# Polynomial-sketch attention into a SiLU expert layer: paired sketch projections, column-tiled key-value sums, outer products on GpSimd

## The chip, the cores and the metric

One core of a Trainium2 chip runs the whole program. The metric is the device time of one execution in microseconds, and the profile is that of one execution.

## What is computed

Four batches of four heads, 1088 positions, head size 32. Queries and keys are each projected by two sketches of eight rows, and the outer product of the two makes 64 features. Linear attention over these features gives, per head, a numerator and a denominator; the quotient is the input of a two-layer expert with SiLU between (128 to 2048 to 128). The output is float32, 4352 x 128.

```python
a = np.einsum('rd,bhsd->bhsr', S1, x)
b = np.einsum('rd,bhsd->bhsr', S2, x)
phi = np.einsum('bhsi,bhsj->bhsij', a, b).reshape(*x.shape[:-1], r * r)
...
kv = np.einsum('bhsf,bhsd->bhfd', k_p, v)
z = np.sum(k_p, axis=2)
num = np.einsum('bhsf,bhfd->bhsd', q_p, kv)
den = np.einsum('bhsf,bhf->bhs', q_p, z)[..., None] + 1e-06
...
h = x @ w_in
return ((h / (1.0 + np.exp(-h))) @ w_out).astype(np.float32)
```

## The kernel before

**Tiles.** A batch has 34 blocks of 128 numbers a partition; eight groups of four blocks are the main part, and two blocks per batch are left over and gathered into one rest tile (`xR`) for all batches. `CW` is nine groups of 32 columns, 288.

**Keys** (`key_tasks`, L251). VectorE transposes the loaded keys (`kt`, L258), TensorE multiplies them with the first and the second sketch (`proj` by `mm_set`, L220: four float32 matmuls of 288 columns in four column tiles of 32, all 128 rows), VectorE transposes each result back (`tr`, L272). `outer` (L277) makes the 64 features of each head in bfloat16, on GpSimd for batch 1 and on VectorE for the others. `z` (L284), `zt`, `l2` (L293) and `wm` (L297) turn the sums of the keys into the masked weights `WM` for the denominator. `kv` (L308) sums features times values over positions, 18 matmuls with 128 columns of features as weights and two heads' values of 64 columns as the moving operand; `kvm` (L316) masks the blocks of other heads.

**Queries** (`query_tasks`, L348). Transposes (L358, L361), three projections (first sketch, second sketch, `WM`; L220 again), each transposed back (L378); `scale` (L384 to L387) makes the denominator and divides, `outer` (L393) makes the features. These are transposed by TensorE (`pet`, L407, and a ScalarE copy, L413) for the first half of batch 0, and by DMA on SP's queue (`dmat`, L399) for the rest. `num` (L422) multiplies by the key-value block, and ScalarE copies the result into the expert's input (`xcopy`, L429).

**Expert** (`moe_tasks`, L488). 68 steps: `h` (L499, 1024 columns into a pair of PSUM banks), `silu` on ScalarE (L503), `o` (L510, accumulated over the steps of a block of positions), then a VectorE transpose and stores. The steps are 4, 4 and 8 for batch 0, 8 for the four-group blocks, 4 for the two-group blocks, and 4 for the rest.

**Order.** A planner (`Plan`) is given each piece of work with an engine, a cost in microseconds, what it depends on, the bank or buffer it takes and gives back, and a due time; expert step n is due at T0 + STEP x n. It simulates the engines once while the program is built and emits the pieces in the order in which they start, so each engine's queue has a fixed order. Two PSUM banks are for attention (`att`), two for expert outputs (`o`), and two pairs for expert inputs (`h`), which batch 0's projections borrow.

**Idle matmuls.** 24 pieces of two matmuls on zeros (`idler`, L542, 256 columns) are in the plan with a late due time and a cost of 0.3 us, so they go where TensorE would have nothing ready.

**Loads.** Batch 0's keys and queries come on SP's queue, its values, the expert weights and all of batches 1 to 3 on GpSimd's.

Of the kernel before, what the change touches and what calls it, by code (L numbers as in the profile page):

```python
# [12 lines left out]
ALU = mybir.AluOpType  # L13
# [9 lines left out]
class Plan:  # L23
# [11 lines left out]
    def add(self, eng, cost, fn, deps=(), take=None, give=None, ready=0.0, due=None, lag=0.0):  # L35

        t = dict(eng=eng, cost=cost, fn=fn, deps=[d for d in deps if d is not None], take=take,
                 give=give, ready=ready, due=due, lag=lag, succ=[], end=None, floor=self.floor, n=len(self.tasks))
        for d in t["deps"]:
            d["succ"].append(t)  # L40
        self.tasks.append(t)
        return t

    def give(self, t, taker, *others):

        t["deps"] += others
        for d in others:
            d["succ"].append(t)
        t["give"] = taker
# [4 lines left out]
    def start_of(self, t, now):  # L54
        if any(d["end"] is None for d in t["deps"]):
            return None
        at = max([t["ready"], now.get(t["eng"], 0.0)]
                 + [d["end"] + self.hop(d, t) for d in t["deps"]])
        if t["take"]:
            if not self.free[t["take"]]:  # L60
                return None
            at = max(at, min(self.free[t["take"]])[0])
        return at

    def run(self, stretch=1.3):
# [9 lines left out]
        while left:  # L75
# [8 lines left out]
            args = ()  # L84
            if t["take"]:
                slot = min(self.free[t["take"]])
                self.free[t["take"]].remove(slot)
                t["slot"] = slot[1]
                args = (slot[1],)
            t["start"], t["end"] = at, at + t["cost"]  # L90
            now[t["eng"]] = t["end"]
            if t["give"]:
                self.free[t["give"]["take"]].append((t["end"] + 0.2, t["give"]["slot"]))
            left.remove(t)
            t["fn"](*args)

@with_exitstack
def kernel(
# [31 lines left out]
    xp = ctx.enter_context(tc.tile_pool(name="xp", bufs=1))  # L130
    gp = ctx.enter_context(tc.tile_pool(name="gp", bufs=1))
# [39 lines left out]
    WAB = const.tile([P, 2, H, R], FP32, name="WAB")  # L171
# [17 lines left out]
    nc.gpsimd.memset(WAB, 0.0)
# [14 lines left out]

    WA = WAB[:, 0].rearrange("p h r -> p (h r)")
    WB = WAB[:, 1].rearrange("p h r -> p (h r)")
    WB4 = const.tile([P, 4, HR], FP32, name="WB4")
    nc.vector.tensor_copy(out=WB4, in_=_bc(WB, 0, 4))
    L2 = const.tile([P, P], FP32, name="L2")

    xT = [xp.tile([P, 1024], BF16, name=f"xT{b}") for b in range(B)]
    xR = xp.tile([P, B, XN], BF16, name="xR")


    T0, STEP = 13.5, 1.2
    pl = Plan({"att": 2, "h": 2, "o": 2, "g": 6})

    def mm_set(dst, srcT, w, lo, hi):
        for c in range(4):
            nc.tensor.matmul(dst[32 * c: 32 * (c + 1), lo:hi], w, srcT[:, c, lo:hi],  # L220
                             start=True, stop=True, tile_position=(0, 32 * c))

    slots = {"h": [ps.tile([P, 2, 512], FP32, name=f"H{i}") for i in range(2)],
             "o": [ps.tile([P, 512], FP32, name=f"O{i}") for i in range(2)],
             "att": [ps.tile([P, 512], FP32, name=f"A{i}") for i in range(2)],
             "g": [gp.tile([P, 2, 512], BF16, name=f"G{i}") for i in range(6)]}
    POOLED = (1,)
# [3 lines left out]
    def bank(pool, i):  # L231
        return slots[pool][i][:, 0, :] if pool == "h" else slots[pool][i]

    def load(b):
        def lk():
            Kx[b] = tile_x(b, "Kx")
            load_x(nc.gpsimd, Kx[b], k, b, 0, SA)

        def lq():
            Qx[b] = tile_x(b, "Qx")  # L240
            load_x(nc.gpsimd, Qx[b], q, b, 0, SA)
        p = b - 2
        at = {1: (14.0, 16.0, 18.0)}.get(b, (0.0, 0.0, 0.0))
        ks[b]["lk"] = pl.add("POOL", 0.6, lk, [ks[p]["kt"][-1] if p >= 0 else None], lag=3.0, due=4.0 + b)
        qs[b]["lq"] = pl.add("POOL", 0.6, lq, [qs[p]["tr"][-1] if p >= 0 else None], lag=3.0, due=4.1 + b)
        ks[b]["lv"] = pl.add("POOL", 2.2, lambda: load_v(b), [ks[p]["kv"] if p >= 0 else None], lag=4.0, due=4.2 + b)
        if b == 1:
            for st, nm, r in ((ks, "lk", 14.0), (qs, "lq", 16.0), (ks, "lv", 18.0)):
                st[b][nm]["lag"] = r - 8.0

    def key_tasks(b):  # L251
        st = ks[b]
        KT = KTs[b % 2]
        at = ((3.9, 4.7) if b == 0 else (0.0, 0.0))

# [6 lines left out]
        def proj(i, sl=None):  # L262
            if b == 0:
                sl = pr[0]["slot"]
            st[f"p{i}"] = slots["h"][sl][:, i, :] if b == 0 else bank("att", sl)
            mm_set(st[f"p{i}"], KT, (WA, WB)[i], 0, CW)

        def tr(i):
            if i == 0:
                st["ab"] = work.tile([P, 2, NBX, HR], FP32, name="kab", tag="kab")  # L270
                st["kp"] = work.tile([P, NBX * H, R, R], BF16, name="kp", tag="kp")
            nc.vector.transpose(out=st["ab"][:, i].rearrange("p a r -> p (a r)"), in_=st[f"p{i}"][:, 0:CW])  # L272

        def outer(lo, hi):
            a = st["ab"][:, 0, lo:hi, :].rearrange("p a (h r) -> p (a h) r", h=H)
            bb = st["ab"][:, 1, lo:hi, :].rearrange("p a (h r) -> p (a h) r", h=H)
            (nc.gpsimd if b in POOLED else nc.vector).tensor_tensor(out=st["kp"][:, H * lo: H * hi], in0=_bc(a, 2, R),  # L277
                in1=_bc(bb, 1, R), op=ALU.mult)

        def z(sl):  # L280
            st["z"] = bank("att", sl)
# [19 lines left out]
        def kv(lo, hi, sl=None):  # L301
            if lo == 0:
                st["kvp"] = bank("att", sl)
            kpf = st["kp"].rearrange("p (t g) i j -> p t (g i j)", g=H)
            for hp in range(2):
                for t in range(lo, hi):
                    n = P if t < NB else XN
                    nc.tensor.matmul(st["kvp"][:, 64 * hp: 64 * (hp + 1)],  # L308
                                     kpf[:n, t, 128 * hp: 128 * (hp + 1)],
                                     Vb[b][:n, 2 * hp: 2 * hp + 2, t, :],  # L310
                                     start=(t == 0 and hp == 0), stop=(t == NB),
                                     skip_group_check=True)

        def kvm():
            st["KV"] = work.tile([P, 2, 2, D], BF16, name="KV", tag="KV")
# [32 lines left out]
    def query_tasks(b, spans, pe=False, at=0.0, groups=None):  # L348
# [94 lines left out]
        if pe:  # L443
            pl.give(ab[1], pr[0], ab[0])
# [156 lines left out]
```

## Time and profile before

| | before |
|---|---|
| median of 3 runs | 111.0 us (110.92 to 111.31) |
| the profiled execution | 111.13 us |
| its span | 108.8 us |
| TensorE busy | 96.6 us |
| ScalarE busy | 72.5 us |
| VectorE busy | 57.0 us |
| GpSimd busy | 20.3 us |
| mean granted TensorE clock | 0.961 |

The span runs from the first to the last instruction of the core; the rest of an execution's time lies around it. In rows of the trace, PE is TensorE's matmuls, PEld its weight loads, DVE is VectorE, ACT ScalarE, POOL GpSimd, and SP the queue of SyncE. L220 is line 220 of the kernel. A float32 matmul has two records, so a set of four is x8. The ends of matmuls are modelled, and neighbouring ones overlap.

### The profile page before, as it was taken

To read this page: it belongs to the slowest core of one execution; us is meant where nothing else is said; L and a number is where in the kernel's file an instruction comes from. 1 tells how busy PE (TensorE), PEld (TensorE's weight loads), DVE (VectorE), ACT (ScalarE), POOL (GpSimd) and SP (SyncE) were. 2 spreads that over 40 slices of the span, in tenths; PEclk is the share of its full clock that TensorE was granted. 3 is DMA by queue.
4 is the path that set the end of the run, shared out by engine and by line. 5 is a ranking of instruction groups with operands and counts; after the bars stand their busy time and mean duration, and the time that the engine had idled before them with its cause. 6 is when DMAs were issued, how large, how long until landed. Compare 5 with 4: busy or idle time off the path is not lost.

```text
span 108.8 us, 2049 instructions
## 1 busy us (share of the span) xinstructions
PE 96.6 (89%) x771; PEld 50.7 (47%) x771; DVE 57.0 (52%) x119; ACT 72.5 (67%) x90; POOL 20.3 (19%) x43
## 2 busy tenths in 40 slices
PE   0797982999999999999999999999999999989920
PEld 0574751644466533443245334433444444778810
DVE  4631799779879999853686039468710200210110
ACT  4200003553379399978968969786979999999910
POOL 4899022451592430000000000000000000000000
PEclk9999998558999999999999999999999999999996
DMA  1999999899641199224009930600555160051243
GB/s 31 305 181 178 164 353 262 176 195 393 185 68 24 38 147 136 52 31 65 3 0 156 98 65 0 96 0 0 108 83 110 19 96 0 12 85 18 34 58 44
DMA packets 32713, 11.08 MB, mean 102 GB/s; under 512 B 29248, under 2 KB 31296, under 8 KB 32704
## 3 DMA queue, kind: packets, MB, share of 16 engines
q1 hardware_dynamic: 26768, 5.38, 30.4%
q0 software_dynamic: 5376, 5.51, 24.7%
q10 hardware_dynamic: 560, 0.07, 0.4%
q8 instruction: 6, 0.10, 0.4%
q14 instruction: 3, 0.02, 0.1%
HBM read 8.78 MB, written 2.23 MB: 101 GB/s over the span
## 4 chain that ended last, share of the span: by engine, by line
PE 72%; ACT 11%; DVE 8%; issue 2%; DMA 1%; POOL 0%; ACTq 0%; POOLq 0%
PE H_147 L499 14%; PE O_149 L510 12%; PE H_146 L499 11%; PE O_148 L510 10%; PE A_151 L220 6%; PE O_148 L542 5%; PE A_150 L220 4%; ACT G_152 L503 3%; PE A_151 L308 2%; DVE kp L277 2%; PE A_150 L422 2%; ACT G_156 L503 2%; ACT G_153 L503 2%; ACT G_157 L503 2%; ACT G_154 L503 2%
## 5 line engine op out<-in xcount | busy, mean ns | idle before, releaser
L499 PEld LDWEIGHTS <-w_in 128*128 128x128 bf16 x176 | 16.1, 101 | 16.4 <-issue 7.7
L510 PEld LDWEIGHTS <-w_out 128*128 128x128 bf16 x176 | 16.5, 98 | 14.3 <-issue 3.5
L503 ACT ACTIVATE G_154<-H_147 128x1024 bf16<-128x1024 f32 x11 | 11.4, 1036 | 4.9 <-PE H_147 L499 4.8
L503 ACT ACTIVATE G_152<-H_147 128x1024 bf16<-128x1024 f32 x12 | 12.6, 1047 | 2.1 <-PE H_147 L499 2.1
L503 ACT ACTIVATE G_156<-H_147 128x1024 bf16<-128x1024 f32 x11 | 11.4, 1036 | 3.0 <-PE H_147 L499 2.8
L503 ACT ACTIVATE G_155<-H_146 128x1024 bf16<-128x1024 f32 x11 | 11.4, 1034 | 2.5 <-PE H_146 L499 2.5
L503 ACT ACTIVATE G_153<-H_146 128x1024 bf16<-128x1024 f32 x12 | 12.6, 1048 | 0.5 <-PE H_146 L499 0.5
L393 DVE TENSOR_TENSOR qp<-aqs,qabm 128x1024 bf16<-128x1024 f32 (+2 forms) x13 | 11.7, 912 | 0.2
L503 ACT ACTIVATE G_157<-H_146 128x1024 bf16<-128x1024 f32 x11 | 11.5, 1042 | 0.0
L152 POOL DMA_DIRECT2D Vb<-in_v_dram x16 | 8.9, 575 | 9.0 <-PE A_151 L308 3.4
L515 DVE STREAM_TRANSPOSE ot<-O_149 128x256 f32<-128x256 f32 (+1 forms) x6 | 3.5, 582 | 13.2 <-PE O_149 L510 13.2
L515 DVE STREAM_TRANSPOSE ot<-O_148 128x512 f32<-128x512 f32 (+1 forms) x5 | 3.0, 609 | 10.8 <-PE O_148 L510 10.8
L542 PE MATMUL O_148<-zero 128*128 128x256 bf16 x48 | 8.2, 337 | 0.0
L277 DVE TENSOR_TENSOR kp<-kab 128x1280 bf16<-128x1280 f32 (+1 forms) x6 | 8.0, 1341 | 0.0
L378 DVE STREAM_TRANSPOSE qabm<-A_151 128x288 f32<-128x288 f32 (+1 forms) x7 | 3.1, 445 | 6.8 <-PE A_151 L220 6.8
L542 PEld LDWEIGHTS <-zero 128*128 128x128 bf16 x48 | 5.7, 125 | 2.0 <-issue 0.4
L290 ACT ACTIVATE zt<-A_150 128x32 f32<-128x32 f32 x1 | 0.2, 197 | 8.7 <-PE A_150 L284 8.7
L499 PE MATMUL H_147<-xT_141,w_in 128*128 128x256 bf16 (+1 forms) x24 | 5.7, 358 | 0.0
L277 POOL TENSOR_TENSOR kp<-kab 128x512 bf16<-128x512 f32 (+1 forms) x5 | 4.9, 1012 | 3.1 <-DVE kab L272 3.1
L499 PE MATMUL H_146<-xT_141,w_in 128*128 128x256 bf16 (+1 forms) x24 | 5.3, 334 | 0.0
L499 PE MATMUL H_147<-xT_144,w_in 128*128 128x256 bf16 (+1 forms) x24 | 4.8, 307 | 0.4 <-ACT G_156 L503 0.4
L499 PE MATMUL H_147<-xT_143,w_in 128*128 128x512 bf16 x16 | 4.8, 382 | 0.2 <-ACT G_156 L503 0.2
(124 smaller groups left out, 151.1 us busy)
## 6 DMA issues: line engine op xcount, KB each, us to landing
Kx<-in_k_dram POOLq DMA_DIRECT2D x3, 544.0 KB, 9.4
Qx<-in_q_dram POOLq DMA_DIRECT2D x3, 544.0 KB, 4.2
out_dram<-ot SPq DMA_DIRECT2D x24, 64.0 KB, 2.0
Vb<-in_v_dram POOLq DMA_DIRECT2D x8, 72.0 KB, 4.6
Vb<-in_v_dram POOLq DMA_DIRECT2D x8, 64.0 KB, 3.9
w_in<-in_moe_w_in_dram POOLq DMA_DIRECT2D x1, 512.0 KB, 7.8
w_out<-in_moe_w_out_dram POOLq DMA_DIRECT2D x1, 512.0 KB, 10.4
out_dram<-ot SPq DMA_DIRECT2D x14, 32.0 KB, 2.9
```

What stands on the lines that cost most here:

```text
L152: nc.gpsimd.dma_start(t[32 * c: 32 * (c + 1), :, 0:n].rearrange("p h a d -> p h (a d)"), AP(tensor=v.tensor, offset=v[b, 0].offset + KA[c] ...
L220: nc.tensor.matmul(dst[32 * c: 32 * (c + 1), lo:hi], w, srcT[:, c, lo:hi], start=True, stop=True, tile_position=(0, 32 * c))
L277: (nc.gpsimd if b in POOLED else nc.vector).tensor_tensor(out=st["kp"][:, H * lo: H * hi], in0=_bc(a, 2, R), in1=_bc(bb, 1, R), op=ALU.mult)
L308: nc.tensor.matmul(st["kvp"][:, 64 * hp: 64 * (hp + 1)], kpf[:n, t, 128 * hp: 128 * (hp + 1)], Vb[b][:n, 2 * hp: 2 * hp + 2, t, :], start= ...
L378: nc.vector.transpose(out=st["abm"][:, i, lo:hi].rearrange("p a r -> p (a r)"), in_=st[f"p{i}", lo0][:, 32 * lo: 32 * hi])
L393: nc.vector.tensor_tensor(out=qp, in0=_bc(st["aqs"][:, H * lo: H * hi], 2, R), in1=_bc(bq, 1, R), op=ALU.mult)
L422: nc.tensor.matmul(ps[64 * hp: 64 * (hp + 1), :n], kst["KV"][:, hp].rearrange("p h d -> p (h d)"), rhs, start=True, stop=True, tile_positi ...
L499: nc.tensor.matmul(view(cc[jp], i), w_in[:, j * P: (j + 1) * P], x, start=True, stop=True)
L503: nc.scalar.activation(out=cc["g", jp], in_=cc[jp], func=ACT.Silu)
L510: nc.tensor.matmul(cc["o"][:, :n], w_out[:, j, :], view(cc["g", jp], i), start=(j == 0), stop=(j == NJ - 1))
L515: nc.vector.transpose(out=cc["ot"][:, :n], in_=cc["o"][:, :n])
L542: nc.tensor.matmul(slots["o"][idle[1]["slot"]][:, 0:256], zero[:, 0:P], zero[:, 0:256], start=True, stop=True)
```

## The change

- `pairs` replaces the two sketch projections. The weights `WP` hold, for each of two halves of 64 rows (two heads), both sketches of these heads in 32 columns. Eight matmuls of 64 rows and 32 columns are placed at row tile 64p and column tile 32c, and each half p writes a bank of its own. `unpair` transposes one such bank back and writes it into the places of both sketches. The third query projection (`projm`) stays as it was.
- `kv` has the values as weights (32 columns of one head) and 64 columns of features as the moving operand, in four column tiles of 32: 36 matmuls. `kvm` masks the result into two copies, `kvt` turns it round by a TensorE transpose, and `kvc` copies it to SBUF, on ScalarE for batch 0 and on VectorE otherwise.
- `outer` of the keys runs on GpSimd for batches 1, 2 and 3, in five pieces each.
- Attention and expert outputs share four PSUM banks (`s`); a piece may take several. Batch 0's projections use these too.
- Keys and queries of batches 2 and 3 are loaded by SP's queue; their loads are ordered behind the last DMA transpose of the batch two before, and so are the loads of values on GpSimd's queue.
- The plan is made first and emitted afterwards. Idle matmuls are no longer pieces of the plan: `emit` puts them into each planned gap of TensorE up to the planned start of the first expert matmul.
- T0 goes from 13.5 to 14.0, STEP from 1.2 to 1.1. The preparation of the weights moves partly between VectorE and GpSimd.

```diff
+    def emit(self, fill=None, until=0.0):
+        last = 0.0
+        for t in self.tasks:
+            if t["eng"] == "PE":
+                if fill and last < until:
+                    fill(last, min(t["start"], until))
+                last = t["end"]
+            t["fn"](*t["slot"])
...
+    zero = const.tile([P, 256], BF16, name="zero")
     nc.gpsimd.memset(S12, 0.0)
+    nc.vector.memset(zero, 0.0)
...
     for h in range(H):
-        (nc.vector if h < 2 else nc.gpsimd).tensor_copy(
-            out=WAB[D * h: D * (h + 1), :, h, :], in_=ST[:, 0:2 * R].rearrange("p (n r) -> p n r", n=2))
+        nc.vector.tensor_copy(out=WP[D * h: D * (h + 1), :, h % 2, :],
+                              in_=ST[:, 0:2 * R].rearrange("p (n r) -> p n r", n=2))
+        nc.gpsimd.tensor_copy(out=WB4[D * h: D * (h + 1), :, h, :], in_=_bc(ST[:, R:2 * R], 0, 4))
...
-    T0, STEP = 13.5, 1.2
-    pl = Plan({"att": 2, "h": 2, "o": 2, "g": 6})
+    T0, STEP = 14.0, 1.1
+    pl = Plan({"h": 2, "s": 4, "g": 6})
...
+    def pairs(dst, srcT, lo, hi):
+
+        for c in range(4):
+            for p in range(2):
+                nc.tensor.matmul(dst[p][32 * c: 32 * (c + 1), lo:hi], WPf[64 * p: 64 * (p + 1), :],
+                                 srcT[64 * p: 64 * (p + 1), c, lo:hi],
+                                 start=True, stop=True, tile_position=(64 * p, 32 * c))
+
+    def unpair(dst, src, p, lo, hi, cut=0):
+
+        nc.vector.transpose(
+            out=dst[:, 0:2, lo:hi, 2 * R * p: 2 * R * (p + 1)].rearrange("p n a g -> p a n g"),
+            in_=src[:, 32 * lo: 32 * hi])
...
+            ks[b]["lk"] = pl.add("SP", 0.5, lk, [ks[p]["kt"][-1], qs[p]["dm"]], lag=4.0)
+            qs[b]["lq"] = pl.add("SP", 0.5, lq, [qs[p]["tr"][-1], qs[p]["dm"]], lag=4.0)
+            ks[b]["lv"] = pl.add("POOL", 2.2, lambda: load_v(b), [ks[p]["kv"], qs[p]["dm"]], lag=4.0)
...
+        def kv(sl):
+            st["kvp"] = bank[sl]
+            kpf = st["kp"].rearrange("p (t h) i j -> p t h (i j)", h=H)
+            for t in range(NBX):
+                n = P if t < NB else XN
+                for h in range(H):
+                    nc.tensor.matmul(st["kvp"][D * h: D * (h + 1), 0: R * R], Vb[b][:n, h, t, :],
+                                     kpf[:n, t, h, :], start=(t == 0), stop=(t == NB),
+                                     tile_position=(0, D * h))
...
+            st["kvx"] = work.tile([P, 2, R * R], BF16, name="kvx", tag="kvx")
+            nc.vector.tensor_tensor(out=st["kvx"], in0=_bc(st["kvp"][:, 0: R * R], 0, 2),
+                                    in1=_bc(pmask[:, :], 1, R * R), op=ALU.mult)
+
+        def kvt():
+            st["kvb"] = st["kvp"].bitcast(BF16)[:, 512: 512 + P]
+            nc.tensor.transpose(st["kvb"], st["kvx"].rearrange("p g f -> p (g f)"), identb)
...
+        pr = pl.add("PE", 0.55, proj, st["kt"], take=("s", "s"))
...
+        k1 = st["kv"] = pl.add("PE", 0.6, kv, ou + [lv], take=("s",), ready=10.0 if b == 0 else 0.0)
...
+    K0CUTS = [("DVE", 0, 5), ("DVE", 5, 9)]
+    KPOOL = [("POOL", i, min(i + 2, NBX)) for i in range(0, NBX, 2)]
...
     pl.run()
+    t1 = first_h[0]["start"]
+
+
+    idle = slots["h"][1][:, 1, 0:256]
+
+    def fill(lo, hi):
+        step = 0.22 if lo < 5.0 else 0.115
+        for _ in range(max(0, int((hi - max(lo, 1.0) - 0.1) / step))):
+            nc.tensor.matmul(idle, zero[:, 0:P], zero, start=True, stop=True)
+
+    pl.emit(fill, t1)
```

## Rows read from the trace of the kernel before

**Rows 1.** The page: busy time by engine, and the granted clock in 40 slices.

```profile
PE 96.6 (89%) x771; PEld 50.7 (47%) x771; DVE 57.0 (52%) x119; ACT 72.5 (67%) x90; POOL 20.3 (19%) x43
...
PEclk9999998558999999999999999999999999999996
```

**Rows 2.** Windows of 1 us: stretch, length, busy PE, PEld, DVE, ACT, POOL, clock, DMA.

```profile
18.00:19.00 1.00, 0.30 (x2) 0.11 (x1) 0.93 (x3) 0.56 (x2) 0.03 (x1) 0.71 1.18 258
...
24.00:25.00 1.00, 1.00 (x12) 0.43 (x4) 0.97 (x4) 0.82 (x1) 0.17 (x1) 0.50 1.05 391
25.00:26.00 1.00, 1.00 (x11) 0.21 (x10) 0.90 (x4) 0.00 (x0) 0.35 (x1) 0.88 0.98 370
```

**Rows 3.** The chain that ended last, in order of time: start, us, what.

```profile
3.98 5.61 PE O_148 L542 x32
...
19.25 0.61 PE O_148 L407 x4
...
28.83 0.44 PE A_151 L284 x18
...
29.31 0.69 PE A_150 L220 x8
...
35.66 0.84 PE A_151 L308 x18
36.50 0.54 PE H_147 L499 x2
37.03 0.43 PE H_146 L499 x2
37.47 0.62 PE A_150 L220 x8
38.09 0.48 PE A_151 L220 x8
...
58.62 0.84 PE A_151 L308 x18
...
100.83 0.87 ACT G_157 L503
```

**Rows 4.** Timeline of the start: start, length, engine, line, what, idle before.

```profile
4.20 1.39 DVE L258 STREAM_TRANSPOSE KT_88<-Kx 128x576 f32<-128x576 f32 x2 [0.75 <-DMA Kx<-in_k_dram]
...
11.57 0.48 DVE L272 STREAM_TRANSPOSE kab<-H_146 128x288 f32<-128x288 f32 x1 [0.81 <-PE H_146 L220]
...
17.58 0.60 ACT L413 ACTIVATE qt<-O_149 128x512 bf16<-128x512 bf16 x1 [4.43 <-PE O_149 L407]
...
19.65 1.06 PE L499 MATMUL H_147<-xT_141,w_in 128*128 128x256 bf16 x4
```

**Rows 5.** Windows of the idle matmuls (L542) alone: busy PE, PEld, clock, DMA.

```profile
5.50:7.50 2.00, 2.00 (x11) 1.44 (x10) 1.00 1.19 206
...
8.00:9.60 1.60, 1.58 (x14) 1.13 (x11) 1.00 0.92 160
```

**Rows 6.** Windows of ScalarE alone: stretch, length, busy time, clock, DMA.

```profile
26.00:40.00 14.00, 8.82 (x12) 1.00 0.52 117
...
sum 83.05, ACT 68.99; mean ACT 11.50
```

**Rows 7.** Timeline, outer products of keys on GpSimd and VectorE, and two of queries.

```profile
28.44 4.92 POOL L277 TENSOR_TENSOR kp<-kab 128x512 bf16<-128x512 f32 x5 [3.09 <-DVE kab L272]
...
29.02 0.78 DVE L393 TENSOR_TENSOR qp<-aqs,qabm 128x256 bf16<-128x256 f32 x1
...
40.30 0.38 DVE L393 TENSOR_TENSOR qp<-aqs,qabm 128x256 bf16<-128x256 f32 x1
40.60 2.62 DVE L277 TENSOR_TENSOR kp<-kab 128x1280 bf16<-128x1280 f32 x2
```

**Rows 8.** DMA issues: KB each, median us from issue to landing.

```profile
Kx<-in_k_dram POOLq DMA_DIRECT2D x3, 544.0 KB, 9.4
...
qt<-qp SPq DMA_TRANSPOSE x11, 3.1
```

More of the change, by code (lines that the diff above doesn't have):

```diff
@@ L56, in start_of @@
             return None
[L57 to L60, printed above, removed]
+        at = max([t["ready"], now.get(t["eng"], 0.0)] + [d["end"] + self.hop(d, t) for d in t["deps"]])
+        for pool in set(t["take"]):
+            n = t["take"].count(pool)
+            if len(self.free[pool]) < n:
                 return None
-            at = max(at, min(self.free[t["take"]])[0])
+            at = max(at, sorted(self.free[pool])[n - 1][0])
         return at
@@ L299, in wm @@
                                     in1=_bc(hmask[:, :], 1, R), op=ALU.mult)
[L301 to L312, printed above, removed]
@@ new lines, in key_tasks @@
+        st["pr"] = [pr]
+        tt = [pl.add("DVE", 0.52, lambda p=p: tr(p), [pr], give=[(pr, p)]) for p in range(2)]
+        st["tr"] = tt
+        ou = [pl.add("POOL", 0.1 + 0.55 * (hi - lo), lambda lo=lo, hi=hi: outer(nc.gpsimd, lo, hi), tt) if e == "POOL"
+              else pl.add("DVE", 0.19 + 0.267 * (hi - lo), lambda lo=lo, hi=hi: outer(nc.vector, lo, hi), tt)
+              for e, lo, hi in kp_cuts]
+        tz = pl.add("PE", 0.38, z, tt, take=("s",))
+        t = pl.add("ACT", 0.22, zt, [tz])
@@ L433, in query_tasks @@
         st.setdefault("tr", []).append(t)
-        pr = []
-        for i in range(3):
-            take = "att" if not pe else ("h" if i == 0 else None)
-            deps = [t] + pr[:1] + ([kst["wm"]] if i == 2 else []) + ([kst["tr"][0]] if pe and i == 2 else [])
-            pr.append(pl.add("PE", 0.16 + 0.04 * nn,
-                             (lambda sl, i=i: proj(i, sl)) if take else (lambda i=i: proj(i)), deps, take=take))
-        st["pr"] = st.get("pr", []) + pr
-        ab = [pl.add("DVE", 0.22 + 0.033 * nn, lambda i=i: back(i, lo0, hi0), [pr[i]],
-                     give=pr[i] if not pe else None) for i in range(2)]
@@ L443, in query_tasks @@
[L443 to L451 removed]
+        pr = pl.add("PE", 0.16 + 0.045 * nn, proj, [t], take=("s", "s"))
@@ new lines, in query_tasks @@
+        pm = pl.add("PE", 0.16 + 0.04 * nn, projm, [t, kst["wm"]], take=("s",))
+        st["pr"] = st.get("pr", []) + [pr, pm]
+        ab = [pl.add("DVE", 0.22 + 0.033 * nn, lambda p=p: back(p), [pr], give=[(pr, p)]) for p in range(2)]
+        for g, (glo, ghi) in enumerate(groups):
+            n = ghi - glo
+            m = pl.add("DVE", 0.22 + 0.033 * n, lambda lo=glo, hi=ghi: backm(lo, hi), [pm, ab[0]],
+                       give=[(pm, 0)] if ghi == hi0 else [])
+            if g:
+                m["deps"].append(bm)
+                bm["succ"].append(m)
+            bm = m
+            sc = pl.add("DVE", 0.72 + 0.12 * n, lambda lo=glo, hi=ghi: scale(lo, hi), ab + [m])
@@ L530, in moe_tasks @@
         pl.add("SP", 0.5 * nst, lambda: store(cc["ot"]), [t], due=due + 6 * STEP)
-    l2p = bank("o", 1)
-    nc.tensor.transpose(l2p[:, 0:P], WB4.rearrange("p c r -> p (c r)"), ident)
-    nc.scalar.activation(out=L2, in_=l2p[:, 0:P], func=ACT.Copy)
-    NF = 24
-    idle = [None]
-    def idler(sl=None):
-        for _ in range(2):
-            nc.tensor.matmul(slots["o"][idle[1]["slot"]][:, 0:256], zero[:, 0:P], zero[:, 0:256],
-                             start=True, stop=True)
-    for i in range(NF):
-        t = pl.add("PE", 0.3, idler, [idle[-1]], take="o" if i == 0 else None, ready=1.0, due=1e5)
-        idle.append(t)
```

234 lines of the change are left out of this document (99 added, 135 removed).

## The prediction, made before the change was run

> **What bounds the kernel now.** I read the page's busy table first [rows 1]: TensorE is busy for 89% of the span, and its granted clock is not at full in one place, slices 7 to 9. Windows of 1 us place that dip [rows 2]: the clock falls within the microsecond at 18 us to 0.50, which is the 1.2 GHz level, with TensorE busy for only 0.30 us of that microsecond, and is back at 2.4 GHz from about 25.2 us (0.88 as the mean of that microsecond).
>
> Then the chain of waits [rows 3]. It has three parts. Up to 19.25 us it is a start-up of one batch. From 19.25 to about 85 us it is TensorE, piece behind piece: an expert step of two 512-column matmuls takes 0.43 us for each of its two layers, and the attention work of later batches stands between. At the end it is ScalarE, one silu of 1024 columns each 0.87 us plus an issue gap, 0.92 us a step, and behind the last silu some 5 us of matmul, transpose and store up to 108.8 us.
>
> The start is read in the timeline [rows 4]. The first key transposes end at 5.59 us, but the key projection starts at 9.59 us, where the fillers end (3.98 + 5.61 [rows 3]). In between TensorE works off 32 idle matmuls on zeros that the plan had put there at 0.15 us each. The windows of that line alone show why they overran [rows 5]: a window counts each matmul that touches it, so up to two too many, and still there are 11 in 2.0 us before 7.5 us (0.2 us each) and 14 in 1.6 us after 8 us (0.11 us each). So this start loses 3.7 us to its own filler, and after the last filler there is a gap in which the clock is lost.
>
> ScalarE has room in the middle: 8.82 of 14.0 us busy from 26 to 40 us, and 68.99 of the 83.05 from its first silu to its last [rows 6]. So time saved on TensorE between 19 and 85 us comes off the end.
>
> **The change part by part.** The profiled execution took 111.13 us with a span of 108.8 us; the median shown is 111.0, so I subtract 0.1 at the end.
>
> *Start.* The filler is now emitted from the finished plan: each planned gap of TensorE before the first expert matmul gets (gap - 0.1)/step matmuls, with a step of 0.22 us in the gap that begins before 5 us and 0.115 us later. Before the key projection, planned at about 5.8 us from the costs in the code, these are 21 matmuls; at 0.2 us each from about 1.2 us they end by 5.7 us, where the key transposes end (5.59) [rows 4]. The projection then starts 3.7 us earlier than at 9.59. Both its sets come out of one piece, so the second key transpose ends some 1.7 us after the start, where now it ends 2.5 us after it (12.05 against 9.59) [rows 3, 4]: another 0.7. Against this the key-value sum of batch 0 now goes through a mask, a TensorE transpose (0.61 us for four [rows 3], 0.15 each) and a ScalarE copy in line with the copy of 0.60 us at 17.58 [rows 4]; I take 0.3. So by waits alone the first expert matmul would move from 19.65 to 15.5 us. But the filler holds TensorE to the plan's pace: going through the plan's costs by hand I get key transposes to 7.7 us, query transposes and outer products on VectorE to 11.4, the first scaled query product to 13.4, its transposes and copy to 15.0, numerator and copy to 16.2, and a first expert matmul at about 16.4. Gain 3.3 us (bounds 0, if filler overruns again, and 4.1, the waits alone).
>
> *Clock.* If TensorE has filler in each gap, it doesn't come to the first expert matmul after a stretch of near idleness, and what now runs at half rate from 19.25 to 25.2 us (6.0 us) would take 3.0 to 3.5 us. Gain 2.6 us (0 if the dip stays, 3.0 at most).
>
> *Projections.* A set today is four fp32 matmuls in four column tiles; alone it takes 0.62 us on the chain, directly behind another set 0.48 [rows 3]. Two sets make both sketches. After, eight matmuls each use 64 rows and 32 columns, so the same number of matmuls as in two sets, but with two of them able to run in one column group. The nearest rows bound it: 0.62 for all eight (as four tiles already share one 0.62), and 1.10 if the two row halves wait for each other. I take 0.70, near the lower end, because in the one row that has tiles sharing a time, they share all of it. The six pairs of batches 1 to 3 (three of keys, three of queries) cost 2 x 1.10 + 3 x 1.24 + 1.31 = 7.2 us now, since only two have the sets back to back, and 4.2 after; with the switch of 0.11 us (0.54 against 0.43 behind a small piece [rows 3]) saved in some of them, 3.2 us. Bounds 0 (as many matmuls as now, so not less) and 3.8. The third set of a query group, with the masked sums as weights, stays.
>
> The Trainium skill, TensorEngine Tiling (Array Packing), Key Properties, says that tiles load and multiply independently; by it a pair would be 0.62 us. No row of this kernel shows row tiles.
>
> *Key-value sums.* Now 18 matmuls of 64 columns under 128-column weights, 0.84 us [rows 3]. After, 36 matmuls of 64 columns in four column tiles, with 32-column weights. The nearest row is the sum z: 18 small ones in column tiles in 0.44 us, 24 ns each [rows 3]; 36 of these are 0.88. Bounds 0.45 (if only half as many slots count) and 1.7 (47 ns each, as now). Then one transpose (0.15) and one more piece to switch to (0.11). Three batches: 3 x 0.30 = 0.9 us of loss; bounds -0.4 and 3.
>
> That page says in the same section that a change of tiling mode drains TensorE, which speaks against this part: the sums leave the 128-column mode of the expert matmuls. The trace doesn't put the cost there: the 0.54 us stands behind the key-value sums too [rows 3], which are in that mode today. By the rule the sums would pay up to 0.14 (0.62 against 0.48) at either side, 0.8 us more in three batches; by the row nothing.
>
> *Outer products.* Those of batches 2 and 3 leave VectorE (2.62 us a batch) for GpSimd (4.92 us a batch) [rows 7]. Costed at nothing: the key-value sum of batch 2 starts 20 us after its key projections end in the trace (58.62 against 38.57 [rows 3]), and GpSimd is busy for only 19% of the span [rows 1]. If that cover went, the price is 2.3 us a batch. Beside GpSimd's product a VectorE product of 256 columns took 0.78 us and 0.38 alone [rows 7]; VectorE is half idle [rows 1], so nothing is taken for that either, nor for its copy of the key-value block.
>
> *Loads.* Keys and queries of batches 2 and 3 move from GpSimd's queue to SP's, behind the last DMA transpose of two batches before. Behind a load that waits on SP stand stores and later DMA transposes; a load of keys needs 9 us to land in the median, a transpose 3 [rows 8]. Key work of batch 2 starts at 37.47 us now [rows 3], and its first expert step comes no sooner than 32 steps of 0.92 us behind the first, near 46 us. By the start above, batch 0's DMA transposes are through by about 26 us, so a load that leaves then lands by 35 and costs nothing; beyond some 3 us of lateness, each microsecond late is one lost.
>
> *Banks.* Two banks for attention and two for expert outputs become four shared ones; the total is the same, and TensorE's order is made by the plan that counts them. Costed at nothing here; its price is rival 3.
>
> Sum: 3.3 + 2.6 + 3.2 - 0.9 = 8.2 us off 111.13, so 102.9, and 102.8 beside the median. ScalarE allows it: between first silu and last it idles about 14 us of 83 [rows 6], and 4.9 of this are used.
>
> **Rivals.**
> 1. *Row halves wait for each other.* The change then doesn't do what it says; the 3.2 goes: 106.0. For it: no row shows row tiles. Against: column tiles do share. Chance 0.15.
> 2. *The start slips.* A filler count worked out from planned times is a wait like the one now: some 50 fillers after 5.8 us (10.6 us to 16.4, less about 4.5 us of other pieces and margins) are planned at 0.115, and if the array still gives one per 0.2 us there, each adds 0.09, 4.5 us in all; or a gap remains and the clock falls as now. Start and half the clock gain go: 107.4. For it: the fillers of now overran by 3.7 us in this way. Against: the rate in the trace rises some 4 us after the fillers begin, by that before 5.8. Chance 0.16.
> 3. *Slower: the shared banks stall TensorE.* A pair must take two of four banks at once, while an expert output holds one for eight steps. Its place is each attention piece, eight in a batch, 24 in three. TensorE issues in order, so expert matmuls queue behind. At 0.34 us a piece the 8.2 are gone; at 0.5 it is 12 us and 114.8. Against: VectorE, which empties the banks, loses work, and the plan counts banks. Chance 0.06.
> 4. *Better than the sum.* Earlier attention lets ScalarE run closer to its 0.92 us a step in the middle: two more of its idle microseconds, 100.5. Chance 0.13.
>
> **Numbers.** Forecast 0.50. Its own range, with each term part of the way to its bounds (start 0.8 more or 1.5 less, sums 0.9 less or 0.7 more, pairs 0.4), is 100.8 to 105. The range goes from 99.5 (rival 4 with its spread) to 107.5 (rivals 1 and 2), which leaves out the slower case, both losses together and the far ends. Faster by over 0.5%: 0.89, as rivals 1, 2 and 4 are faster too, though part of 2 with part of 1 would end level (0.04 same); slower 0.07. A measurement of this kernel can tell about 0.5% from no change.
>
> **What the profile after would show.** Key projection starting near 5.9 us; first expert matmul by 16.5; no 0.50 in the clock after that; a pair piece of 16 matmul records at about 0.70 us on the chain; key-value sums near 0.88; ScalarE less idle from 26 to 80 us. Pairs at 1.1 us, a first expert matmul after 18 us, or waits of TensorE for VectorE's transposes out of the banks would prove this wrong.

## The result, and the profile after

The changed kernel took 105.2 us (median) beside 111.0 for the kernel before on the same chip: a ratio of 0.940 [0.926, 0.954]. A second series of it gave 105.5 us, 0.949 [0.939, 0.958]. Medians count every execution, while ratios and their intervals leave out those that took over 1.5% more than the fastest of the same kernel, so 105.2 and 111.0 do not give 0.940. Between the medians the gain is 5.8 us (6.6 by the ratio) where 8.2 were forecast; 105.2 lies inside the range of 99.5 to 107.5. The profiled execution took 104.95 us with a span of 103.2.

The page, busy time and granted clock, beside [rows 1]:

```profile
PE 92.5 (90%) x862; PEld 49.7 (48%) x871; DVE 52.1 (50%) x121; ACT 73.3 (71%) x91; POOL 28.1 (27%) x52
...
PEclk9999999995999999999999999999999999999996
```

The dip of slices 7 to 10 [rows 1] has shrunk to one, slice 10, and it begins 4 us later (22.7 us where it was 18.4), no longer ahead of the first expert matmul but 7 us behind it. The timeline of the start shows what came before, to be held against [rows 4] and the fillers in [rows 3]; then VectorE and ScalarE around the dip:

```profile
1.06 4.66 PE L574 MATMUL H_147<-zero 128*128 128x256 bf16 x21 [1.06 <-DVE pmask L183]
5.66 0.43 PE L227 MATMUL B_148<-KT_84,WP 64*32 64x288 f32 x1
15.61 0.60 PE L501 MATMUL H_146<-xT_141,w_in 128*128 128x256 bf16 x4
...
18.84 1.37 DVE L263 STREAM_TRANSPOSE KT_85<-Kx 128x576 f32<-128x576 f32 x2 [3.11 <-DMA Kx<-in_k_dram]
20.19 1.25 DVE L359 STREAM_TRANSPOSE QT_87<-Qx 128x1024 f32<-128x1024 f32 x1
21.49 0.30 DVE L233 STREAM_TRANSPOSE qabm<-B_148 128x160 f32<-128x160 f32 x1
21.85 0.43 PE L227 MATMUL B_148<-KT_85,WP 64*32 64x288 f32 x1 [2.14 <-DVE qabm L233]
23.80 1.02 ACT L505 ACTIVATE G_156<-H_146 128x1024 bf16<-128x1024 f32 x1 [3.50 <-PE H_146 L501]
```

The 21 fillers now end at 5.72 us, the key projection starts at 5.66, and the first expert matmul at 15.61, 4.0 us earlier than the 19.65 of before. Some 4 us later TensorE meets a new stall. VectorE has to empty the banks of batch 0's second query pair (L233, the bank B_148), but the transposes of batch 1's keys and queries stand ahead of that in its order, and the first of them waits 3.11 us for the load of the keys. TensorE's next piece needs that bank and waits 2.14 us; ScalarE waits 3.50 us for the expert step behind it. Windows of 1 us, in the columns of [rows 2]:

```profile
20.00:21.00 1.00, 0.00 (x0) 0.00 (x0) 1.00 (x2) 0.30 (x1) 0.00 (x0) 1.00 0.20 27
21.00:22.00 1.00, 0.15 (x1) 0.13 (x2) 1.00 (x5) 0.00 (x0) 0.00 (x0) 1.00 0.04 9
22.00:23.00 1.00, 1.00 (x18) 0.39 (x17) 0.92 (x4) 0.00 (x0) 0.00 (x0) 0.87 0.00 0
23.00:24.00 1.00, 1.00 (x7) 0.69 (x6) 0.91 (x3) 0.20 (x1) 0.00 (x0) 0.50 0.00 0
...
26.00:27.00 1.00, 1.00 (x10) 0.86 (x9) 0.45 (x1) 0.69 (x2) 1.00 (x2) 0.93 0.83 158
26.00:40.00 14.00, 12.56 (x151) 6.24 (x151) 9.89 (x19) 10.22 (x13) 7.66 (x10) 0.99 0.95 175
```

TensorE is idle from 19.7 to 21.85, and the clock is at the 1.2 GHz level from about 22.7 to 26.1 (the means of 0.87 and 0.93 place its ends): half of those 3.4 us, 1.7, is lost too. Together with the wait of 2.1 that is an estimated 3.8 us given back in this execution. Not every execution loses clock: the other three of the series had a mean granted clock of 0.998 to 1.000 and took 105.45, 105.75 and 103.52 us. In the profiled one ScalarE then has 10.22 us of work in 26 to 40, against 8.82 [rows 6]. The chain that ended last shows the load and the changed pieces:

```profile
7.59 11.23 DMA Kx<-in_k_dram
...
28.59 0.36 PE B_151 L227
...
28.99 0.20 PE B_151 L227
...
29.24 0.34 PE B_148 L296 x2
...
35.16 4.65 DMA qt<-qp
...
71.54 0.49 PE B_148 L310 x36
72.03 0.32 PE H_146 L501
...
72.40 0.59 PE B_151 L512 x2
...
74.01 0.16 PE B_148 L321
74.17 0.43 PE H_146 L501 x2
```

A pair of sketches runs from 28.59 to 29.24, 0.65 us (its records are split on the chain; the 0.56 of two expectations below, 0.36 + 0.20, leaves out the gaps between them), where two sets took 1.10 [rows 3]. The key-value sums take 0.49 against 0.84, their transpose 0.16. TensorE's waits (us in total, times, longest):

```profile
PE B_148 L227 <- DVE qabm L233: 2.1, 1, 2.1
...
PE B_150 L428 <- DMA qt<-qp: 0.9, 1, 0.9
```

### The profile page after: what moved, and what is told of

Its sections match the earlier page's. It is cut to its first block, busy times and chain, and to the rows that moved or that the text cites. A ratio compares the mean times of both kernels' runs of the same rounds, so it can differ in the third digit from the quotient of the medians.

```text
span 103.2 us, 2255 instructions
## 1 busy us (share of the span) xinstructions
PE 92.5 (90%) x862; PEld 49.7 (48%) x871; DVE 52.1 (50%) x121; ACT 73.3 (71%) x91; POOL 28.1 (27%) x52
## 4 chain that ended last, share of the span: by engine, by line
PE 44%; DMA 22%; ACT 14%; DVE 6%; POOL 5%; issue 4%; DVEq 0%; ACTq 0%; POOLq 0%
DMA Kx<-in_k_dram 11%; DMA qt<-qp 10%; PE H_146 L501 9%; PE H_147 L501 9%; PE B_151 L512 6%; PE B_149 L512 6%; PE B_150 L512 4%; ACT G_153 L505 3%; ACT G_155 L505 3%; ACT G_152 L505 2%; ACT G_156 L505 2%; PE B_148 L512 2%; POOL Vb L153 2%; ACT G_154 L505 2%; ACT G_157 L505 2%
## 5 line engine op out<-in xcount | busy, mean ns | idle before, releaser
L280 POOL TENSOR_TENSOR kp<-kab 128x512 bf16<-128x512 f32 (+1 forms) x15 | 14.4, 987 | 35.5 <-DVE kab L233 35.5
L512 PEld LDWEIGHTS <-w_out 128*128 128x128 bf16 x176 | 17.4, 100 | 13.0 <-issue 1.2
L574 PE MATMUL H_147<-zero 128*128 128x256 bf16 x72 | 11.7, 316 | 1.1 <-DVE pmask L183 1.1
L574 PEld LDWEIGHTS <-zero 128*128 128x128 bf16 x72 | 7.7, 113 | 3.6 <-DVE pmask L183 1.1
L263 DVE STREAM_TRANSPOSE KT_85<-Kx 128x576 f32<-128x576 f32 (+1 forms) x4 | 2.8, 724 | 5.0 <-DMA Kx<-in_k_dram 5.0
L501 PE MATMUL H_147<-xT_141,w_in 128*128 128x256 bf16 (+1 forms) x24 | 5.2, 333 | 0.1
L501 PE MATMUL H_146<-xT_141,w_in 128*128 128x256 bf16 (+1 forms) x23 | 5.0, 332 | 0.3 <-ACT G_154 L505 0.3
L501 PE MATMUL H_147<-xT_142,w_in 128*128 128x512 bf16 x16 | 4.8, 380 | 0.1
L517 DVE STREAM_TRANSPOSE ot<-B_150 128x256 f32<-128x256 f32 (+1 forms) x2 | 1.2, 584 | 7.2 <-PE B_150 L512 7.2
L501 PE MATMUL H_146<-xT_144,w_in 128*128 128x256 bf16 (+1 forms) x24 | 4.8, 308 | 0.0
L501 PE MATMUL H_147<-xT_143,w_in 128*128 128x512 bf16 x15 | 4.6, 379 | 0.1
L501 PE MATMUL H_146<-xT_143,w_in 128*128 128x512 bf16 x15 | 4.6, 381 | 0.0
## 6 DMA issues: line engine op xcount, KB each, us to landing
Kx<-in_k_dram POOLq DMA_DIRECT2D x1, 544.0 KB, 11.2
```

Source lines behind the costliest of these rows:

```text
L263: nc.vector.transpose(out=KT[:, lo:hi, 0: 32 * n], in_=Kx[b][:, KA[lo]: KA[hi], :].rearrange("p (c a) d -> p c (a d)", c=hi - lo))
L280: eng.tensor_tensor(out=st["kp"][:, H * lo: H * hi], in0=_bc(a, 2, R), in1=_bc(bb, 1, R), op=ALU.mult)
L501: nc.tensor.matmul(view(cc[jp], i), w_in[:, j * P: (j + 1) * P], x, start=True, stop=True)
L512: nc.tensor.matmul(cc["o"][:, :n], w_out[:, j, :], view(cc["g", jp], i), start=(j == 0), stop=(j == NJ - 1))
L517: nc.vector.transpose(out=cc["ot"][:, :n], in_=cc["o"][:, :n])
L574: nc.tensor.matmul(idle, zero[:, 0:P], zero, start=True, stop=True)
```

## The experiments

All ratios are to the kernel before; diffs are against the changed kernel unless it is said otherwise.

**Was it the order on VectorE, or the late load?** The planner believes that batch 1's keys land 7.5 us after their issue, and so puts their transposes (L263) ahead of batch 0's last ones out of the banks. Experiment e1_lag only tells it a later landing; the load itself stays as it is:

```
-  ks[b]["lk"] = pl.add("POOL", 0.6, lk, lag=7.5, due=4.0)
-  qs[b]["lq"] = pl.add("POOL", 0.6, lq, lag=9.0, due=4.1)
-  ks[b]["lv"] = pl.add("POOL", 2.2, lambda: load_v(b), lag=9.0, due=4.2)
+  ks[b]["lk"] = pl.add("POOL", 0.6, lk, lag=18.0, due=4.0)
+  qs[b]["lq"] = pl.add("POOL", 0.6, lq, lag=18.5, due=4.1)
+  ks[b]["lv"] = pl.add("POOL", 2.2, lambda: load_v(b), lag=18.0, due=4.2)
```

> The changed kernel, in which only the plan's belief about batch 1's loads is corrected: keys, queries and values land at about 18 us in the plan (7.5 to 9 us before). The loads themselves leave as they did; the plan then puts VectorE's transposes out of the banks for the second half of batch 0 ahead of batch 1's key transposes. Theory A (order): the changed kernel loses time because VectorE waits at 15.7 to 18.8 us for batch 1's keys with those bank transposes queued behind, and TensorE behind these; so TensorE's idle time at 19.7 to 21.9 us and the fall of the clock behind it go, and the time is about 101.5 us, 0.915 of before. Theory B (late data): batch 1's work is late whatever the order, TensorE idles a little later, and the time stays within 1 us of the changed kernel, 104.2 to 105.7, 0.94 to 0.95.

Measured: 102.3 us, 0.916 [0.908, 0.925]. VectorE's timeline, windows of all engines, then the page's clock and TensorE's longest wait (the profiled execution took 103.54 us, the longest of four):

```profile
18.02 0.58 DVE L233 STREAM_TRANSPOSE qabm<-B 128x160 f32<-128x160 f32 x2 [1.51 <-PE B L227]
...
21.42 1.36 DVE L263 STREAM_TRANSPOSE KT<-Kx 128x576 f32<-128x576 f32 x2
```

```profile
19.00:23.00 4.00, 4.00 (x38) 3.43 (x36) 3.86 (x8) 4.00 (x6) 0.00 (x0) 1.00 0.06 12
22.00:27.00 5.00, 5.00 (x78) 3.04 (x75) 3.88 (x9) 3.43 (x5) 1.71 (x2) 1.00 0.34 64
```

```profile
PEclk9999999999999998599999999999999999999999
```

```profile
PE B L428 <- DMA qt<-qp: 1.3, 1, 1.3
```

The banks are emptied at 18.02 and the keys transposed at 21.42, without a wait for the load; up to 27 us TensorE is busy throughout and the clock is at full. It falls later here, near 40 us, behind a wait of 1.3 us for a DMA transpose. The load leaves as before and 2.9 us come back, so the order is what made the late load costly (the plan orders everything anew with this edit, so it is the worth of the order as a whole). The profile alone would not show it: in it the keys landed after 9.1 us, 2 us sooner than in the changed kernel's first profile.

Experiment e2_sp1 keeps that order on VectorE and brings the data early: batch 1's keys and queries go on SP's queue, right behind batch 0's.

```
-  load_x(nc.gpsimd if b == 1 else nc.sync, Kx[b], k, b, 0, SA)
+  load_x(nc.sync, Kx[b], k, b, 0, SA)
...
-  ks[b]["lk"] = pl.add("POOL", 0.6, lk, lag=7.5, due=4.0)
+  ks[b]["lk"] = pl.add("SP", 0.5, lk, lag=7.5, due=4.0)
```

(and the same two edits for the queries.)

> The changed kernel with batch 1's keys and queries loaded by SP's queue right behind batch 0's, the order of the compute engines unchanged. Theory A (order) and B (late data) both expect the wait at 15.7 us gone if the keys land before 16 us, and about 101.5 us, 0.915. A rival C (the DMA engines are full from 2 to 18 us, as their busy share near 1 says): something else lands later by what these land earlier, batch 0's values or the expert's first weights, the first expert matmul slips by 1 to 3 us, and the time is 103 to 106.

Measured: 101.2 us, 0.914 [0.907, 0.921], the fastest of all, though not to be told from e1_lag. Its timeline, then its chain:

```profile
15.99 1.33 DVE L263 STREAM_TRANSPOSE KT<-Kx 128x576 f32<-128x576 f32 x2
...
16.52 1.04 PE L501 MATMUL H<-xT,w_in 128*128 128x256 bf16 x8
...
18.49 0.54 DVE L233 STREAM_TRANSPOSE qabm<-B 128x160 f32<-128x160 f32 x2
```

```profile
5.50 6.83 DMA Vb<-in_v_dram
12.46 0.56 PE B L310 x36
20.62 0.65 PE B L227 x16
...
31.98 4.14 DMA qt<-qp
```

The keys are there at 15.99, and the clock does not fall at this place or behind it. It has a price of its own: batch 0's values land at 12.33, the key-value sum waits 0.5 us for them, and the first expert matmul starts at 16.52, 0.9 later than in the changed kernel's first profile. Experiment e14_sp1_vfirst tried to win that back by issuing the values ahead of GpSimd's four copies of the sketch (diff against e2_sp1):

```
-      nc.gpsimd.tensor_copy(out=WB4[D * h: D * (h + 1), :, h, :], ...
   load_v(0)
+  for h in range(H):
+      nc.gpsimd.tensor_copy(out=WB4[D * h: D * (h + 1), :, h, :], ...
```

> The kernel with batch 1's loads on SP's queue (0.914), with GpSimd issuing the loads of batch 0's values and of the expert weights before its four copies of weights instead of behind them, 0.9 us earlier. Theory: the key-value sum of batch 0 waited 0.5 us for values in that kernel, so 0.3 to 0.6 us faster, 0.908 to 0.911, the fastest of all. Rival: the plan's fillers hold TensorE, nothing gained, 0.914.

Measured: 101.8 us, 0.920 [0.912, 0.928]: no gain. The wait for the values is gone from TensorE's list, and yet the first expert matmul starts at 16.54, as in e2_sp1 (16.52): those 0.5 us were not what held the start.

**The changed kernel once more.** Run after_again has no edit.

> The changed kernel once more, on the chip of these runs, so that the others are set against it: 0.94, between 103.5 and 105.8 us, the spread coming from how late batch 1's keys land.

Measured: 105.5 us, as given above. Here the load took 9.9 us and VectorE waited 1.32 us for it; TensorE's waits:

```profile
PE B L428 <- DMA qt<-qp: 2.6, 1, 2.6
...
PE B L227 <- DVE qabm L233: 0.6, 1, 0.6
```

So the stall at L227 varies with the landing of one load (2.1 us in the first profile, 0.6 here), and a second loss shows. The DMA transpose of batch 1's first query products, issued at 32.54, took 6.33 us to land (the median is 3.1 in [rows 8]); TensorE waited 2.6 us for it, and behind that wait the clock falls too:

```profile
38.00:39.00 1.00, 0.08 (x2) 0.08 (x1) 0.84 (x1) 0.00 (x0) 1.00 (x2) 0.89 1.29 257
39.00:40.00 1.00, 1.00 (x4) 0.29 (x4) 0.00 (x0) 0.41 (x1) 1.00 (x2) 0.50 0.09 16
```

In e2_sp1 that transpose took 4.14 us and TensorE waited 0.4. The kernel before has no wait of TensorE for a DMA transpose in its list.

**The filler.** Experiment e7_nofill emits no fillers behind the first gap:

```
 def fill(lo, hi):
-    step = 0.22 if lo < 5.0 else 0.115
+    if lo > 5.0:
+        return
+    step = 0.22
```

> The changed kernel without the filler matmuls behind the first gap (those before 5.7 us stay). Theory: the filler behind the key projection keeps the clock at 2.4 GHz for the start; without it the clock falls before or at the first expert matmul, and the time grows by 1.5 to 3 us, 107 to 108, 0.965 to 0.975. Rival: it buys nothing, since the clock falls later anyway, and TensorE's short pieces are not on the path of the start: 104.5 to 105.5, 0.94 to 0.95.

Measured: 108.0 us, 0.980 [0.971, 0.988], 2.8 us above the median with them (3.1 and 3.9 points above the two ratios). Clock on the page, and windows:

```profile
PEclk9999555699999997599999999999999999999999
```

```profile
15.00:21.00 6.00, 5.67 (x48) 3.08 (x49) 3.71 (x6) 3.58 (x7) 0.00 (x0) 0.54 0.76 186
```

Without filler the stretch from about 10.5 to nearly 21 us (slices 5 to 8) runs at the lower level, as the one from 18 to 25 us did before the change [rows 2]. At a mean clock of 0.54, the 5.67 us in which TensorE is busy there lose about 2.6 us (5.67 x 0.46), which is the forecast's clock term. The 2.8 us at the end are a net figure: this profile has no wait of TensorE for the banks (it gets there later, at half rate), but one of 3.5 us for the DMA transpose, behind which the clock falls a second time (slices 16 and 17):

```profile
PE B L428 <- DMA qt<-qp: 3.5, 1, 3.5
```

**The start alone.** Experiment e8_before_start is the kernel before with a mended start: idle matmuls 256 wide from the beginning and planned at 0.44 us a pair, and the transpose of the sketch moved behind the first key projection. Diff against the kernel before:

```
+  zero = const.tile([P, 256], BF16, name="zero")
+  nc.vector.memset(zero, 0.0)
...
-  t = pl.add("PE", 0.3, idler, [idle[-1]], take="o" if i == 0 else None, ready=1.0, due=1e5)
+  t = pl.add("PE", 0.44, idler, [idle[-1]], take="o" if i == 0 else None, ready=1.0, due=1e5)
```

> The kernel before with its start alone repaired: fillers planned at 0.44 us a piece of two instead of 0.30, the zeros cleared first, and the transpose that waited for the weights until 3.5 us moved behind the first key projection. Nothing else of the change. Theory: this gives the start and the clock part of the forecast, the first expert matmul near 16.3 us instead of 19.65 and no fall of the clock before it, 3.3 + 2.6 us less whatever the wait for batch 1's keys takes back (0 to 2): 105 to 107, 0.945 to 0.965. Rival: the gain of the change comes from its projections and key-value sums, and the start is hidden by batch 1's late keys: 108.5 to 110, 0.98 to 0.995.

Measured: 109.8 us, 0.992 [0.988, 0.996]. The start was mended only in part: the clock still falls in it (slices 4 and 5), and the first expert matmul came at 18.04, not near 16.3. Of these 1.6 us, 0.9 were left at the end. The chain names a load of batch 1 again, and a DMA transpose of 7.62 us behind it, for which TensorE waits 1.7 us. The page's clock, the first expert matmul, and the chain:

```profile
PEclk9997699999999999999999999999999999999995
```

```profile
18.04 1.04 PE L503 MATMUL H<-xT,w_in 128*128 128x256 bf16 x8
```

```profile
7.94 12.33 DMA Qx<-in_q_dram
...
24.59 7.62 DMA qt<-qp
```

Experiment e13_before_start_sp1 puts batch 1's loads on SP's queue in that kernel (the edit of e2_sp1).

> The kernel before with its start repaired (run alone: 0.992) and, in addition, batch 1's keys and queries on SP's queue right behind batch 0's. Theory: the repaired start was given back because VectorE's bank transposes for the second half of batch 0 stand behind batch 1's query transpose, which waited for data until 20.3 us; with the data early, the 1.6 us of start and the 2.6 us of clock show: 105.5 to 107, 0.955 to 0.97. Rival: the old projections and banks bound the middle whatever the start, and it stays at 0.985 to 0.995.

Measured: 107.3 us, 0.968 [0.958, 0.978]. The windows of 26 to 40 us, e8_before_start and then e13_before_start_sp1, and the latter's first expert matmul:

```profile
26.00:40.00 14.00, 11.97 (x114) 6.34 (x106) 11.62 (x21) 8.87 (x12) 6.63 (x9) 1.00 0.78 134
```

```profile
26.00:40.00 14.00, 13.47 (x126) 6.87 (x126) 13.03 (x22) 11.23 (x14) 5.06 (x8) 1.00 0.63 100
```

```profile
16.65 1.04 PE L503 MATMUL H<-xT,w_in 128*128 128x256 bf16 x8
```

ScalarE gets 11.23 us of work in place of 8.87. In the old kernel too, early data for batch 1 let more of an earlier start reach the end. How much is theirs stays open: in this profile the start itself is 1.4 us earlier (16.65) and its clock does not fall, and no run shows whether the moved loads did that.

**The pairs.** Experiment e3_sets goes back to two sets of four 128-row tiles, with the plan unchanged:

```
-  for c in range(4):
-      for p in range(2):
-          nc.tensor.matmul(dst[p][32 * c: 32 * (c + 1), lo:hi], WPf[64 * p: 64 * (p + 1), :],
-                           srcT[64 * p: 64 * (p + 1), c, lo:hi],
-                           start=True, stop=True, tile_position=(64 * p, 32 * c))
+  for p in range(2):
+      for c in range(4):
+          nc.tensor.matmul(dst[p][32 * c: 32 * (c + 1), lo:hi], WS[p], srcT[:, c, lo:hi],
+                           start=True, stop=True, tile_position=(0, 32 * c))
```

> The changed kernel with the two sketches projected by two sets of four 128-row matmuls, as before the change, in the same places of the same order. On the chain a pair took 0.56 us in the changed kernel; two sets back to back took 1.10. Theory: TensorE is what bounds most of the middle, so seven pairs give back 0.5 us each: 3.5 us, 108.7, 0.98 of before. Rival: the changed kernel's middle is bound by waits (keys, DMA transposes), so only some of it shows: 1 to 2 us, 106.5, 0.96.

Measured: 106.2 us, 0.951 [0.940, 0.962], 1 us above the changed kernel and not to be told from it. In its profile TensorE stood at L227 for 0.6 us only, as the keys landed after 9.2 us, so a stall that varies may hide what the pairs are worth. Experiment e9_sp1_sets makes the same edit in e2_sp1.

> The kernel with batch 1's loads on SP's queue (run before this: 0.914), with the projections as two sets of 128 rows again; it takes the wait for batch 1's keys out of the comparison. Theory: a pair takes 0.56 us on the chain against 1.10 for two sets back to back, and TensorE is the bound of the middle; seven pairs make 3.5 us, 104.6, 0.945. Rival: half of it is hidden by waits for DMA transposes and by ScalarE, 102.5 to 103, 0.93.

Measured: 103.3 us, 0.937 [0.933, 0.940]; against e2_sp1 the pairs are worth 2.3 points of the ratio, 2.5 us. Two sets on its chain, where e2_sp1 has a pair of 0.65:

```profile
20.79 1.11 PE B L227 x16
```

**The key-value sums.** Experiment e10_sp1_kv puts the 18 matmuls of before back into e2_sp1, without the transpose and copy:

```
-  for t in range(NBX):
-      for h in range(H):
-          nc.tensor.matmul(st["kvp"][D * h: D * (h + 1), 0: R * R], Vb[b][:n, h, t, :], kpf[:n, t, h, :], ...
+  for hp in range(2):
+      for t in range(NBX):
+          nc.tensor.matmul(st["kvp"][:, 64 * hp: 64 * (hp + 1)], kpf[:n, t, 128 * hp: 128 * (hp + 1)],
+                           Vb[b][:n, 2 * hp: 2 * hp + 2, t, :], ...
```

> The same kernel (batch 1 on SP's queue) with the key-value sums as before the change: 18 matmuls under 128-column weights, no transpose, no copy. On the chain the new sums took 0.49 and their transpose 0.15 us, a piece more to switch to 0.11; the old ones 0.84. Theory: this part of the change is worth nothing within 0.5 us, 100.8 to 101.7, 0.911 to 0.919. Rival: the old sums give a shorter path to the numerator (no transpose, no copy), 0.5 to 1 us faster, 0.905.

Measured: 103.8 us, 0.928 [0.924, 0.932], slower than with the new sums by 1.4 points, some 1.5 us. Its four executions lie apart, at 102.2 and 102.4 us and at 105.3 and 105.6. The profile is of the one of 105.3; in it TensorE waits longer for the DMA transpose:

```profile
PE B L429 <- DMA qt<-qp: 2.5, 1, 2.5
```

The plan's order changes with this edit too (batch 1's queries are transposed at 21.98 us, in e2_sp1 at 17.24). So the 1.5 us cannot be put down to the sums alone, the profile does not explain the shorter executions, and no more is read from this run.

**Loads and outer products.** Experiment e12_sp1_pool returns the loads of batches 2 and 3 to GpSimd's queue, and e11_sp1_dve their key outer products to VectorE, each in e2_sp1:

```
+  ks[b]["lk"] = pl.add("POOL", 0.6, lk, [ks[p]["kt"][-1], qs[p]["dm"]], lag=4.0)
...
-  key_tasks(b, KPOOL)
+  key_tasks(b, KPOOL if b == 1 else K0CUTS)
```

(the first edit is e12_sp1_pool's, with the like for queries; the second is e11_sp1_dve's.)

> The same kernel (batch 1 on SP's queue) with the keys and queries of batches 2 and 3 on GpSimd's queue, as before the change. Theory: behind the loads on SP's queue the first DMA transpose of the next batch lands late (4.65 us in the changed kernel where the median is 3.2), and it stands in the chain; on GpSimd's queue the loads wait behind outer products instead, but there is slack; 0.3 to 0.8 us faster, 0.907 to 0.911. Rival: the loads on GpSimd's queue come 3 us later and TensorE waits for batch 2: slower by 1 to 3 us, 0.92 to 0.94.

> The kernel with batch 1's loads on SP's queue (0.914), with the key outer products of batches 2 and 3 on VectorE again. Theory (the prediction's): worth nothing, both engines have room; 0.910 to 0.919. Rival: VectorE's queue is what the bank transposes wait in, and 2.6 us more of it in one go stalls TensorE; slower by 0.5 to 1.5 us, 0.92 to 0.93.

Measured: e12_sp1_pool 101.7 us, 0.918 [0.911, 0.925], no difference that can be told from e2_sp1. e11_sp1_dve 102.9 us, 0.927 [0.918, 0.935], 1.3 points above e2_sp1 with intervals that still touch. In its profile, of the longest of its four executions (103.8 us), TensorE waits 2.0 us for the transposed query products and 1.6 for batch 0's values:

```profile
PE B L428 <- DMA qt<-qp: 2.0, 1, 2.0
PE B L310 <- DMA Vb<-in_v_dram: 1.6, 1, 1.6
```

The second of these lies ahead of everything the edit touches, so whether the move to GpSimd gains something stays open.

## Why the prediction was right in its sign and 2.4 us off

**Start, forecast 3.3: 4.0 us at the first expert matmul, 3.6 in after_again (16.09).** The filler did not overrun, and 15.61 is near the end that the forecast called the waits alone, 15.5. Rival 2 falls.

**Clock, forecast 2.6: some 2.6 in e7_nofill's windows.** The 2.8 us at that run's end hold other waits too and do not confirm the size. The cover at the start holds. But the forecast's test, no 0.50 behind the first expert matmul, failed: the clock fell at another place, for another reason.

**Pairs, forecast 0.70 each and 3.2 in all: 0.65 each, and 2.5 us in e9_sp1_sets.** On TensorE the six pairs take 3.9 us (6 x 0.65) where they took 7.2, so 3.3 are freed there. The two row halves shared their time (0.65 for eight matmuls, 0.62 for a set of four), and rival 1 falls. The rule of the Trainium skill, TensorEngine Tiling (Array Packing), Key Properties, that tiles work independently, gave 0.62; the measured 0.65 is nearer to that than to the forecast's 0.70.

**Key-value sums, forecast a loss of 0.9: nearer a gain of 0.6.** This term was mis-sized, and the gain lies beyond the 0.4 that its bounds allowed. The 24 ns of z's row was the wrong neighbour: 36 matmuls took 0.49 us, 13.6 ns each, near the lower bound of 0.45. With the transpose of 0.16 the piece goes from 0.84 to 0.65, 0.2 less in each of three batches, if they are like the one on the chain. The new piece to switch to cost nothing either: behind the transpose an expert step takes its usual 0.43. Behind the sums an expert step takes 0.96 us for both its layers (72.03 to 72.99; one of its four matmul records is missing) against 0.86, about as much more as the 0.11 that already stood behind the old ones. The Trainium skill, TensorEngine Tiling (Array Packing), Key Properties, says that a change of tiling mode drains TensorE. By that rule the sums would have cost up to 0.14 more at either side; the trace shows some 0.10 behind them and no cost that is new.

**Outer products and loads, forecast 0.** For batches 2 and 3 e12_sp1_pool agrees on the loads. Whether GpSimd's outer products cost or gain anything stays open (e11_sp1_dve).

**What failed is a step that isn't there.** "Loads" went through the loads that the change moves, those of batches 2 and 3, and "Banks" was "costed at nothing here". Neither asked whether the load that stays, batch 1's keys, issued at 7.6 us, would still be in time for a start that comes 4 us earlier. It landed at 18.8; VectorE reached it at 15.7, with the transposes that free TensorE's banks queued behind it. That is rival 3's wait, TensorE standing for a bank that VectorE has yet to empty, and one of the signs that the prediction named as proving it wrong; but the rival priced it as 24 small waits that come from having four shared banks, while it is one wait of 2.1 us that comes from VectorE's order, and in the profiled execution it brings a clock loss of 1.7 with it. The runs e1_lag and e2_sp1, by two different edits, take back 2.4 and 2.7 points of the ratio (2.7 and 2.9 us) from the first series, and 3.3 and 3.5 points from the second.

For the first profile the terms can be added up, as an account and not as a proof, since they come from different runs and the pairs gave 2.5 us end to end, not 3.3: 4.0 + 2.6 + 3.3 + 0.6 = 10.5, less the 3.8 of the stall and its clock and 0.9 for the DMA transpose, is 5.8 of gain; the profiled executions differ by 6.2 (111.13 to 104.95). So it was partly luck that the forecast of 8.2 came this near: it left out a loss of 3.8 and took start and sums 2.2 too small (0.7 and 1.5), and the two errors offset each other. The profile of after_again divides its losses otherwise: 0.6 at the banks, 2.6 for the DMA transpose and some 1.7 of clock behind that. What the executions of 105.45 and 105.75 us lost, at full clock, no profile shows.

Still open: why the same load takes 9.1 to 11.2 us on GpSimd's queue from one execution to the next, and why the first DMA transpose of batch 1 takes from 4.14 us (e2_sp1) to 6.33 (after_again) and 7.30 (e7_nofill). Returning the loads of batches 2 and 3 to another queue didn't shorten the latter (5.15 us in e12_sp1_pool).

## What to carry to other kernels

When a start-up is shortened, list every load that the next stage consumes, also those the change doesn't touch, and compare issue plus landing time with the moment at which its consumer is now reached. Where the consumer shares an in-order engine with the instructions that free another engine's buffers, a late load stops both; telling the planner the true landing time was worth about as much here as making the load earlier (0.916 and 0.914). And an edit measured in a kernel with a movable stall (the pairs in e3_sets, the start in e8_before_start) can show too little: take the stall away first.

## What the runs showed of the hardware that was not expected

- Matmuls of 64 columns under 32-column weights, in four column tiles, went through at 13.6 ns each (36 in 0.49 us on the chain of the first profile; 0.56 for batch 0's in e2_sp1), against 24 ns for the small ones of z [rows 3].
- Batch 1's load of keys, 544 KB on GpSimd's queue at about 7.6 us, took 9.1 us to land in e1_lag, 9.9 in after_again and 11.2 in the changed kernel's first profile, the same instruction each time; on SP's queue, issued at 3.1 us, it took 6.2 in e12_sp1_pool. Batch 0's values took 6.83 us in e2_sp1, with that load on SP's queue, where the median of such loads in the changed kernel was 5.5.
- Behind an idle time of TensorE of 2.1 us (20 to 22 us in the first profile) and a wait of 2.6 (after_again) the clock went to the lower level; in e11_sp1_dve it did not behind a wait of 2.0.
